# Weight rows of the first two chunks in even and odd order, and three late chunks in one load, in the opening of a two-problem attention kernel

## Chip, cores, metric

One core of a Trainium2 chip. The metric is the device time of one execution in microseconds (us); the median of several executions is given with its range. "Ratio" is the mean time of one kernel's fast runs over that of the kernel before in the same rounds, so it is not quite the ratio of the medians that are quoted. A profile is one execution, traced; its span is about 1.8 us shorter than the device time. Each ratio is taken within one session; where single traces are compared, they can be of different chips.

## The reference

Two independent problems A and B of one shape; the outputs are put side by side.

```
B, Sq, D = 16, 32, 1024
Hq, Hkv, Sk, Dh = 32, 4, 512, 128          # bf16
q = (x @ wq) as [B, Hq, Sq, Dh]            # wq: 1024 x 4096
scores = q k^T * Dh**-0.5 ; p = softmax(scores) ; o = p v
out = o @ wo                               # wo: 4096 x 1024
```

Only the product `x @ wq` of problem A, for its first eight heads, is touched here. It sums over the 1024 model dimensions in eight chunks of 128. Any assignment of dimensions to chunks gives the same sum, as long as x and wq use the same one.

## The kernel before

TensorE is kept busy nearly all the time by a plan in which scores, values and projections are woven together. What matters here is the opening, before that plan starts: while the first data arrive, eight heads are accumulated chunk by chunk in eight places of PSUM. x comes on two ways: its first 256 dimensions as they are, to be transposed by TensorE, the other 768 by transposing DMA loads.

```python
NF = REP - 2            # six heads first, two after them
HC = DC // 2            # 4 of the 8 chunks
wq_v = A_wq.rearrange("(c p) n -> p c n", p=P)
...
load_x(TT // 2, TT, nc.scalar)
nc.scalar.preload_act_table_set("natural_log_exp_and_others")
load_x(0, TT // 2)
load_w0(0, 1, 0, NF // 2)                  # chunk 0, three heads
load_w0(0, 1, NF // 2, NF, nc.scalar)      # chunk 0, three more
load_w0(1, 2, 0, NF)                       # chunk 1
load_w0(2, 3, 0, NF, nc.scalar)            # chunk 2
load_x_transposed(2)                       # x for chunks 2 and 3
load_w0(3, 4, 0, NF)
load_w0(0, HC, NF, REP)                    # chunks 0 to 3 of the last two heads
load_w0(HC, HC + 1, 0, REP)
load_x_transposed(HC)
load_w0(HC + 1, DC - 1, 0, REP)            # chunks 5 and 6
load_x_transposed(HC + 2)
load_w0(DC - 1, DC, 0, REP)                # chunk 7
...
warm_up(22)                                # matmuls on constants
for k, ts in enumerate(((0, TT // 2), (TT // 2, TT))):
    transpose_x(0, *ts, nc.vector.tensor_copy)
    transpose_x(1, *ts, nc.scalar.copy, spare[k])
for ts in ((0, TT // 2), (TT // 2, TT)):
    first_heads(range(0, NF // 2), (0,), *ts)
first_heads(range(NF // 2, NF), (0,))
first_heads(range(NF), (1, 2, 3))
first_heads(range(NF, REP), range(HC))
first_heads(range(REP), range(HC, DC - 1))
for n, h in enumerate((0, 2, 4, 6, 5, 7, 1, 3)):
    first_heads((h,), (DC - 1,))
    ...                                    # copy head h out of PSUM
```

## Time and profile before

| | kernel before |
|---|---|
| device time, median of the first three runs | 343.4 us (343.21 to 343.67) |
| span of the profiled execution | 341.1 us |
| TensorE busy | 334.5 us, 98% |
| chunk 1 issued, landed | 1.75, 6.23 us |
| first matmul of chunk 1 | 6.28 us |
| first matmul of the next heads (after the opening's 67) | 18.80 us |

How to read it: TensorE is the bound. The opening is the first 19 us. The prediction below shows the lines of the profile of before that carry this. A row of the timeline is start, duration, engine, source line, operation, and in brackets the idle time before it with what ended it.

### The profile page before, as it was taken

How to read it: one execution, taken by the hardware profiler on the slowest of the kernel's cores; microseconds unless marked ns; L12 is line 12 of the kernel's file. 1: busy time of each engine (PE TensorE's matmuls, PEld its weight loads, DVE VectorE, ACT ScalarE, POOL GpSimd, SP SyncE). 2: the span in 40 equal slices, each digit the busy share in tenths (PEclk: the TensorE clock that was granted, in tenths of full speed). 3: DMA queues.
4: the chain of work that ended last, by engine and by line, in shares of the span. 5: the costliest groups of instructions: out<-in, count | busy, mean ns of one | idle time of the engine just before them, and what ended most of it. 6: DMA issues, size and time to landing. Idle time of an engine off the chain costs nothing.

```text
span 341.1 us, 5436 instructions
## 1 busy us (share of the span) xinstructions
PE 334.5 (98%) x2074; PEld 212.8 (62%) x2113; DVE 265.4 (78%) x335; ACT 185.3 (54%) x208; POOL 47.0 (14%) x206
## 2 busy tenths in 40 slices
PE   8999999999999999999999999999999999999996
PEld 5455666666666666666666666666666666666555
DVE  0047988888988898888888988879888888889540
ACT  2057666666667667666645545555554555555110
POOL 0001110011111111110012221222122101111100
PEclk9999999999999999999999999999999999999999
DMA  7999999999996998899999955998449995430001
GB/s 199 298 188 274 288 250 225 205 254 250 301 258 144 241 222 232 197 294 308 322 293 290 240 125 147 338 284 222 118 106 307 357 194 152 115 93 9 17 19 33
DMA packets 128622, 71.70 MB, mean 210 GB/s; under 512 B 76880, under 2 KB 127824, under 8 KB 128592
## 3 DMA queue, kind: packets, MB, share of 16 engines
q1 hardware_dynamic: 127504, 69.78, 82.5%
q0 software_dynamic: 384, 1.05, 0.8%
q10 hardware_dynamic: 704, 0.49, 0.5%
q8 instruction: 17, 0.28, 0.3%
q14 instruction: 13, 0.11, 0.1%
HBM read 50.59 MB, written 2.10 MB: 154 GB/s over the span
## 4 chain that ended last, share of the span: by engine, by line
PE 96%; DMA 2%; issue 1%; ACT 0%; SPq 0%; ACTq 0%
PE f_ps L320 31%; PE q_ps L301 28%; PE ob L425 17%; PE s_ps L357 16%; PE q_ps L531 4%; DMA w_sb<-in_A_wq_dram 1%; DMA out_dram<-o_sb 0%; ACT o_sb L329 0%; SPq L465 0%; SPq L474 0%; ACTq L329 0%; ACT p_sb L365 0%; ACTq L365 0%
## 5 line engine op out<-in xcount | busy, mean ns | idle before, releaser
L365 ACT ACTIVATE p_sb<-s_ps,shift 128x1024 bf16<-128x1024 f32 x128 | 142.7, 1115 | 97.5 <-PE s_ps L357 86.3
L376 DVE TRANSPOSE_TENSOR_REDUCE parts<-p_sb 128x32 f32<-128x1024 bf16 x128 | 158.7, 1240 | 20.8 <-ACT p_sb L365 19.3
L320 PE MATMUL f_ps<-wo_sb,oT 128*128 128x512 bf16 (+1 forms) x524 | 127.6, 366 | 0.6
L301 PE MATMUL q_ps<-xT,wq_sb 128*128 128x512 bf16 x430 | 113.0, 379 | 0.6
L425 PE MATMUL ob<-p_sb,v_sb 128*128 128x256 bf16 x512 | 76.8, 273 | 0.8
L357 PE MATMUL s_ps<-qT,kT 128*128 128x256 bf16 x512 | 76.8, 273 | 0.0
L320 PEld LDWEIGHTS <-oT 128*128 128x128 bf16 x544 | 53.2, 98 | 35.3
L357 PEld LDWEIGHTS <-kT 128*128 128x128 bf16 x512 | 56.9, 113 | 28.3
L301 PEld LDWEIGHTS <-wq_sb 128*128 128x128 bf16 x448 | 43.8, 98 | 32.2
L425 PEld LDWEIGHTS <-v_sb 128*128 128x128 bf16 x512 | 50.1, 98 | 20.0
L447 DVE TENSOR_TENSOR oT<-r,ob 128x512 bf16<-128x512 f32 x64 | 43.9, 686 | 19.8 <-PE ob L425 19.4
L411 DVE STREAM_TRANSPOSE r<-rall 128x512 f32<-128x512 f32 x64 | 44.2, 691 | 1.1
L309 ACT CAST qT<-q_ps 128x512 bf16<-128x512 f32 x56 | 32.7, 583 | 16.5 <-PE q_ps L301 16.5
L394 POOL COPY half<-cs 64x32 f32<-64x32 f32 x32 | 6.6, 206 | 231.5 <-DVE cs L384 231.4
L329 ACT CAST o_sb<-f_ps 128x512 bf16<-128x512 f32 (+1 forms) x17 | 9.5, 559 | 23.6 <-PE f_ps L320 23.6
L531 PE MATMUL q_ps<-xT,w_sb 128*128 128x512 bf16 (+1 forms) x66 | 14.1, 369 | 0.6 <-DMA w_sb<-in_A_wq_dram 0.6
L406 DVE RECIPROCAL rall<-sums 128x32 f32<-128x32 f32 x32 | 10.4, 326 | 3.3 <-POOL sums L403 3.3
L384 DVE TENSOR_REDUCE cs<-parts 128x32 f32<-128x128 f32 x32 | 12.1, 377 | 1.1
L553 DVE CAST qT<-q_ps 128x512 bf16<-128x512 f32 x4 | 2.5, 683 | 13.2 <-PE q_ps L531 13.2
L531 PEld LDWEIGHTS <-w_sb 128*128 128x128 bf16 x67 | 6.4, 97 | 8.0 <-DMA w_sb<-in_A_wq_dram 1.1
L553 ACT CAST qT<-q_ps 128x512 bf16<-128x512 f32 x4 | 2.1, 599 | 12.8 <-PE q_ps L531 12.8
L331 POOL DMA_DIRECT2D out_dram<-o_sb x8 | 4.6, 575 | 29.2 <-ACT o_sb L329 29.2
(25 smaller groups left out, 48.1 us busy)
## 6 DMA issues: line engine op xcount, KB each, us to landing
v_sb<-in_A_v_cache_dram SPq DMA_DIRECT2D x16, 512.0 KB, 5.4
wq_sb<-in_B_wq_dram SPq DMA_DIRECT2D x8, 1024.0 KB, 6.0
wo_sb<-in_A_wo_dram SPq DMA_DIRECT2D x8, 1024.0 KB, 7.5
v_sb<-in_B_v_cache_dram SPq DMA_DIRECT2D x16, 512.0 KB, 4.6
wo_sb<-in_B_wo_dram SPq DMA_DIRECT2D x8, 1024.0 KB, 8.5
wq_sb<-in_A_wq_dram SPq DMA_DIRECT2D x5, 1024.0 KB, 6.7
wq_sb<-in_A_wq_dram SPq DMA_DIRECT2D x2, 512.0 KB, 7.3
kT<-in_A_k_cache_dram SPq DMA_TRANSPOSE x64, 4.4
```

The lines of the kernel that those rows point to most:

```text
L301: nc.tensor.matmul(ps[:], lhsT=w[:, dc, (h % 4) * DH:(h % 4 + 1) * DH], rhs=xT[pr][:, dc, :], start=(dc == 0), stop=(dc == DC - 1),)
L309: nc.scalar.copy(out=qT[pr, g][:, :, hl, :], in_=ps[:].rearrange("p (b s) -> p b s", s=SQ),)
L320: nc.tensor.matmul(ps[:, 0:width], lhsT=oT[pr, tt][:, h, :], rhs=wo_tiles[pr, nh, h // REP][:, h % REP, off:off + width], start=(h == 0), ...
L357: nc.tensor.matmul(s_ps[:, c, :], lhsT=kT[:, i % GRP, c, :], rhs=qT[pr, g][:, b, :, :].rearrange("p h s -> p (h s)"), start=True, stop=True,)
L365: nc.scalar.activation(out=p_sb[:], in_=s_ps[:], func=ACTF.Exp, bias=shift[:], scale=SCALE)
L376: nc.vector.tensor_reduce(out=parts[k][:, q, :, :].rearrange("p c h -> p (c h)"), in_=st[i]["p"][:].rearrange("p c (h s) -> p (c h) s", s=SQ),
L384: nc.vector.tensor_reduce(out=cs[:], in_=parts.pop(k)[:].rearrange("p q c h -> p q h c"), axis=AX.X, op=ALU.add,)
L406: nc.vector.reciprocal(out=rall[:, k, :], in_=quad.pop(k)[:])
L411: nc.vector.transpose(out=r[:].rearrange("p n s -> p (n s)"), in_=rall[:, k, o * 2 * REP:(o + 1) * 2 * REP] .unsqueeze(2).to_broadcast([P, ...
L425: nc.tensor.matmul(ob[j][:, q, :], lhsT=v_sb[:, i % GRP, c, :], rhs=st[i]["p"][:, c, :], start=(c == 0), stop=(c == KC - 1),)
L447: nc.vector.tensor_tensor(out=out, in0=rcp.pop(j)[:].rearrange("p (q h) s -> p q h s", h=REP), in1=ob.pop(j)[:].rearrange("p q (h s) -> p ...
L531: nc.tensor.matmul(first_q[h][:, ts], lhsT=w0[dc // HC][:, dc % HC, h * DH:(h + 1) * DH], rhs=xT[0][:, dc, ts], start=(dc == 0 and t0 == 0 ...
```

## The change

Intent: chunks 0 and 1 take the even and the odd ones of the first 256 dimensions, so that row 2p for chunk 0 and row 2p+1 for chunk 1 are neighbours in memory. x is transposed at a step of 2 to match. Besides, chunks 5, 6 and 7 come in one load, and the load of chunks 0 to 3 of the last two heads becomes two. So the whole program issues 176 DMA transfers before and after.

```diff
+            pair_v = A_wq[0:2 * P].rearrange("(p c) n -> p c n", c=2)
...
             def load_w0(d0, d1, h0, h1, eng=nc.sync):
+                rows = wq_v if d0 >= 2 else pair_v
...
-                    in_=wq_v[:, d0:d1, h0 * DH:h1 * DH],
+                    in_=rows[:, d0:d1, h0 * DH:h1 * DH],
...
-            load_w0(0, HC, NF, REP)
+            load_w0(0, 2, NF, REP)
+            load_w0(2, HC, NF, REP)
             load_w0(HC, HC + 1, 0, REP)
             load_x_transposed(HC)
-            load_w0(HC + 1, DC - 1, 0, REP)
+            load_w0(HC + 1, DC, 0, REP)
             load_x_transposed(HC + 2)
-            load_w0(DC - 1, DC, 0, REP)
...
-                        ps[:, tt * P:(tt + 1) * P], x_sb[:, tt, d * P:(d + 1) * P], ident[:]
+                        ps[:, tt * P:(tt + 1) * P], x_sb[:, tt, d:2 * P:2], ident[:]
```

## The prediction

> **What bounds the kernel now.** I read the page's busy shares and its chain first, then the opening of the program (the diff touches nothing else) as a timeline, then the chain of that stretch, the landings of its loads, and the stretch by windows.
>
> From the page of the kernel before:
>
> ```profile
> PE 334.5 (98%) x2074; PEld 212.8 (62%) x2113; DVE 265.4 (78%) x335; ACT 185.3 (54%) x208; POOL 47.0 (14%) x206
> ...
> PE 96%; DMA 2%; issue 1%; ACT 0%; SPq 0%; ACTq 0%
> ...
> L357 PEld LDWEIGHTS <-kT 128*128 128x128 bf16 x512 | 56.9, 113 | 28.3
> ...
> L425 PEld LDWEIGHTS <-v_sb 128*128 128x128 bf16 x512 | 50.1, 98 | 20.0
> ```
>
> TensorE is busy 98% of 341.1 us and is 96% of the chain that ended last. The change removes no matmul, so only waits of TensorE can be won. DMA is 2% of the chain; part of it is the output's end, the rest lies in the opening. The timeline of the opening (start, duration, engine, line, operation, count, idle before):
>
> ```profile
> 0.93 2.52 PE L513 MATMUL q_ps<-const-bfloat16-1.0 128*128 128x128 bf16 x22 [0.93 <-PEq L687]
> ...
> 1.26 0.92 SPq L474 DMA_DIRECT2D w_sb<-in_A_wq_dram  x2
> ...
> 1.34 0.94 ACTq L474 DMA_DIRECT2D w_sb<-in_A_wq_dram  x2
> 2.22 1.44 SPq L468 DMA_TRANSPOSE xT<-in_A_x_dram  x1
> ...
> 3.40 0.88 PE L521 MATMUL xT_ps<-ident,x_sb 128*128 128x128 bf16 x8
> ...
> 4.17 1.50 PE L531 MATMUL q_ps<-xT,w_sb 128*128 128x256 bf16 x9
> ...
> 6.27 12.20 PEld L531 LDWEIGHTS <-w_sb 128*128 128x128 bf16 x58 [1.09 <-DMA w_sb<-in_A_wq_dram]
> 6.28 12.69 PE L531 MATMUL q_ps<-xT,w_sb 128*128 128x512 bf16 x57 [0.59 <-DMA w_sb<-in_A_wq_dram]
> ```
>
> Chunk 0 of the weights (nine matmuls) is used up early; then TensorE waits once, for chunk 1, and never again in the opening. The 58 weight loads of the last rows belong to 58 matmuls (one record is missing), so one 512-wide matmul takes (12.69 - 0.16)/58 = 0.216 us, where 0.16 is what the last one's 0.38 us of latency has over the pace. The idle row shows 0.59 us against the modelled end of the matmul before. By the pace, the ninth started at 5.30 and its successor could have started at 5.52 instead of 6.28: the true loss is 0.76 us. The chain of the first 9 us says which load that is:
>
> ```profile
> 1.70 0.05 issue
> 1.75 4.48 DMA w_sb<-in_A_wq_dram
> 6.23 0.05 issue
> 6.28 2.33 PE q_ps L531 x10
> ```
>
> It is chunk 1 from the SyncE queue, 192 KB, issued at 1.75 and landed at 6.23. The DMA rows of single issues (KB, us to landing) for chunk 1 with chunk 2, the first transposing load of x (dimensions 2 and 3), and the present load of chunks 5 and 6:
>
> ```profile
> w_sb<-in_A_wq_dram SPq DMA_DIRECT2D x1, 192.0 KB, 4.5
> w_sb<-in_A_wq_dram ACTq DMA_DIRECT2D x1, 192.0 KB, 4.7
> ...
> xT<-in_A_x_dram SPq DMA_TRANSPOSE x1, 5.2
> ...
> w_sb<-in_A_wq_dram SPq DMA_DIRECT2D x1, 512.0 KB, 5.5
> ```
>
> Windows (length, busy time by engine, clock, DMA share, GB/s):
>
> ```profile
> 2.00:4.00 2.00, 2.00 (x20) 1.68 (x19) 0.17 (x1) 0.60 (x1) 0.00 (x0) 1.00 0.89 278
> 4.00:5.60 1.60, 1.60 (x14) 0.94 (x11) 0.41 (x2) 0.65 (x2) 0.00 (x0) 1.00 1.15 220
> 5.60:6.30 0.70, 0.10 (x2) 0.03 (x2) 0.00 (x0) 0.00 (x0) 0.00 (x0) 1.00 0.88 166
> 6.30:9.00 2.70, 2.65 (x12) 1.26 (x14) 0.00 (x0) 0.00 (x0) 0.00 (x0) 1.00 1.14 308
> 9.00:12.00 3.00, 3.00 (x16) 1.37 (x14) 0.00 (x0) 0.00 (x0) 0.00 (x0) 1.00 1.20 298
> ```
>
> The DMA engines have packets in flight all the time (share about 1), but the rate drops from 278 to 220 and 166 GB/s just where chunks 1 and 2 and the first transposing load are in flight. Packets wait there. That is the place the change may touch.
>
> **What the skill says.** (1) "DMA: Bandwidth & Descriptors", section "Issuing engines are not separate DMA queues": DMAs of SyncE and ScalarE interleave on the same 16 engines, only issue time is saved. The trace agrees: chunks 1 and 2, issued within 0.1 us of each other from two queues, land 0.27 us apart, both after over 4.4 us. (2) Same page, "Latency and other measured facts", on the row pitch in HBM at large powers of two: copies at a per-partition pitch of 512 KiB made 207 GB/s, at 2 MiB 164. The change takes the pitch of chunks 0 and 1 from 8 KiB (4096 bf16) to 16 KiB, far below these. The trace has only one pitch for these loads and doesn't settle it. (3) "SBUF — State Buffer", the note on cachelines of 16 bytes: a bf16 step up to 8 should be free. The trace differs slightly: weight loads of kT, read at a step of 4 elements, take 113 ns against 98 ns for v_sb, read in order.
>
> **The change part by part.**
> - Even and odd dimensions. The same 256 rows of wq are read, in the same 128 packets of 768 or 1536 bytes for each load; only which rows belong to which load changes. Even and odd rows stay separate slices of a row, so no packet gets longer. Work removed: none. If neighbouring rows are cheaper for the memory to serve, chunk 1 lands earlier than 6.23. Nothing in the trace measures that.
> - Transposes of x. Eight weight loads from x_sb now read at step 2. At most 113 - 98 = 15 ns each by the kT rows, 8 x 0.015 = 0.12 us, ahead of chunk 0. That delay falls into the 0.76 us wait for chunk 1: 0 on the path.
> - The load of the two last heads of chunks 0 to 3 is split in two: one more issue of about 0.5 us on SyncE (the row of 0.92 for two gives 0.46 each) at about 5 us. By the pace these heads are due at 6.28 + 18 x 0.216 = 10.16 and the load landed at 9.10. 0 on the path.
> - Chunks 5 to 7 in one load: one issue fewer, which gives the 0.5 us back before the next weight loads. But chunk 5 now waits for chunk 7's 256 KB too: 262,144 B at 298 GB/s = 0.88 us, so 12.33 + 0.88 = 13.21, against a need at 6.28 + 34 x 0.216 = 13.62. It holds by 0.41 us; with the extra issue's 0.5 us in full it would be late by about 0.1 us. The third transposing load, behind it, goes from 13.28 to some 14.2, needed at 15.35. Chunk 7 goes from 15.44 to 13.2, needed at 17.08. Nothing of that is won, as it was not waited for.
> - Sum of the sure parts: 0.0 us. The open part is the 0.76 us wait.
>
> **How much of the 0.76 us can be had.** After chunk 1 come six matmuls, so chunk 2 is due at 6.28 + 6 x 0.216 = 7.57. Chunk 2 landed at 6.50, but its x at 7.39 (issued at 2.22, 5.18 us): only 0.18 us of slack. If chunk 1 alone comes early, the gain stops at 0.18 us and the wait moves to xT. For more, the transposing load must come earlier too, which it may if the packets ahead of it in the same queue stall less. Then 0.66 us of slack at chunk 3 (8.21 against 8.87) and 0.41 us at chunks 5 to 7 come next. A gain of 0.4 us would already be a good outcome.
>
> **Rivals.**
> A. Neighbours help: chunk 1 lands by about 5.5, the transposing load advances some. For: the rate dip to 220 and 166 GB/s says that the memory or the queues, and not the bytes, hold it up. Against: all packets are the same size and number, and the dip also coincides with the start of the transposing load, which stays. Time: 342.7 to 343.2.
> B. Nothing moves, or the wait passes to xT after 0.18 us: 343.2 to 343.4. For: the same bytes, queues and order of issue up to 4.8 us.
> C. The wider pitch hurts, or the odd rows collide with chunk 2, which is read beside them: chunk 1 later by 0.3 to 0.5 us, loss one for one: 343.7 to 343.9. For: this wait has no slack at all. Against: 16 KiB is still a small pitch.
> D. Chunks 5 to 7 late by 0.1 to 0.3 us: 343.5 to 343.7.
>
> **Range and chances.** I give A 0.4, B 0.35, C 0.15 and D 0.1. Weighted with 342.95, 343.3, 343.8 and 343.6 the mean is 343.3; as A's gain is what the change is made for, and its tail is longer, I say 343.2 us. The three runs before span 0.46 us by themselves, so the range is 342.5 to 343.9. 2% is 6.9 us; the opening's whole wait is 0.76 us. Faster by over 2%: 0.005; slower: 0.005; within: 0.99.
>
> **What would show it.** In the chain of the first 9 us the DMA piece ahead of the first long run of matmuls tells all: its end at 6.23 moves earlier in A (and a second wait, for xT at about 7.3, appears if only chunk 1 moved), stays in B, is later in C. D shows as an idle of TensorE near 13.6 us. The eight transposes should take 0.88 to 1.0 us. From 24 us on, every row should be the old one shifted by the same amount. I am wrong if the body's pace changes, or if the opening moves by more than 0.8 us.

## The result, and the profile after

343.28 us median of 6 runs (342.95 to 343.62) against 343.31 us of before (342.94 to 343.67, 6 runs); ratio 0.9999, 95% interval 0.9986 to 1.0011. No difference.

The page of the changed kernel, engines and chain, as before:

```profile
PE 335.0 (98%) x2074; PEld 213.2 (62%) x2113; DVE 265.4 (78%) x335; ACT 185.4 (54%) x208; POOL 47.1 (14%) x206
...
PE 96%; DMA 2%; issue 1%; ACT 0%; SPq 0%; ACTq 0%
```

The chain of the first 24 us of the changed kernel (start, duration, what):

```profile
1.75 4.80 DMA w_sb<-in_A_wq_dram
6.56 0.05 issue
6.60 2.33 PE q_ps L533 x10
```

The same load as before sets the start of the long run of matmuls. In this execution it landed at 6.56, 0.33 us later than in the profile of before. From there on every weight load of TensorE is later by 0.327 or 0.328 us: the body of the kernel has no slack and adds no noise.

The timeline of the changed kernel, TensorE's rows of the opening:

```profile
3.40 1.04 PE L523 MATMUL xT_ps<-ident,x_sb 128*128 128x128 bf16 x8
...
4.23 2.03 PE L533 MATMUL q_ps<-xT,w_sb 128*128 128x256 bf16 x9
...
6.60 12.69 PE L533 MATMUL q_ps<-xT,w_sb 128*128 128x512 bf16 x57 [0.34 <-DMA w_sb<-in_A_wq_dram]
```

The 57 recorded matmuls take the same 12.69 us as before. But the nine of chunk 0 took 2.03 us in place of 1.50, and TensorE's idle time before chunk 1 is 0.34 in place of 0.59 us. TensorE was slower, and waited less. This was in no step of the prediction, and it turned out to be half of the story.

The windows of the changed kernel for the stretch in which the rate of the DMA dropped before (columns as in the prediction):

```profile
4.00:5.60 1.60, 1.60 (x12) 1.23 (x10) 0.41 (x2) 0.75 (x2) 0.00 (x0) 1.00 0.92 218
5.60:6.30 0.70, 0.66 (x4) 0.10 (x1) 0.00 (x0) 0.00 (x0) 0.00 (x0) 1.00 1.13 160
```

218 and 160 GB/s against 220 and 166: in this execution the dip is where it was. It is not in every execution, though: in the second looks (next section) the same two stretches moved 287 and 271 GB/s in the changed kernel, 240 and 116 in the kernel before. In the experiments with one part alone it was 238 and 67 with even and odd rows, 241 and 68 with rows in turn. So the dip changes from execution to execution in both forms, and neighbouring rows do not lift it dependably.

### The profile page after: what moved, and what is told of

Same layout as the page of the kernel before. It is cut to its first block, busy times and chain, and to the rows that moved or that the text cites. A ratio compares the mean times of both kernels' runs of the same rounds, so it can differ in the third digit from the quotient of the medians.

```text
span 341.5 us, 5438 instructions
## 1 busy us (share of the span) xinstructions
PE 335.0 (98%) x2074; PEld 213.2 (62%) x2113; DVE 265.4 (78%) x335; ACT 185.4 (54%) x208; POOL 47.1 (14%) x206
## 4 chain that ended last, share of the span: by engine, by line
PE 96%; DMA 2%; issue 1%; ACT 0%; SPq 0%; ACTq 0%
PE f_ps L320 31%; PE q_ps L301 28%; PE ob L425 17%; PE s_ps L357 16%; PE q_ps L533 4%; DMA w_sb<-in_A_wq_dram 1%; DMA out_dram<-o_sb 0%; ACT o_sb L329 0%; SPq L466 0%; SPq L476 0%; ACTq L329 0%; ACT p_sb L365 0%; ACTq L365 0%
```

## The experiments

Theories: (1) neither part of the change touches what sets the end; chunk 1's landing scatters by itself. (2) The change itself delays chunk 1 by 0.3 us. (3) Two effects cancel. Later: what holds chunk 1 up, and what else bounds the opening (theory C, TensorE's pace).

All "full pace" times below are read from the starts of single matmuls in the trace, to about 0.1 us: 512 columns are 0.427 us apart at first ("half pace") and 0.216 us later, and the time is that at which the distance changes.

### Both kernels looked at again

No edit.

> The kernel before, unchanged, looked at once more. Theory 1 (the 0.3 us by which the changed kernel's first chunk-1 load landed later is chance): chunk 1 lands anywhere from 6.1 to 6.7 us, not at 6.23 again, and the first late matmul follows it by 0.05 us. Theory 2 (the change itself delays chunk 1): it lands at 6.2 to 6.3 again. Time 342.9 to 343.7 us either way.

> The changed kernel, unchanged, looked at once more. Theory 1 (chance): chunk 1 lands anywhere from 6.1 to 6.7 us. Theory 2 (the change delays it): 6.5 to 6.6 again. Time 342.9 to 343.7 us.

Measured: 343.25 and 343.36 us, one run each, so of unknown state. The kernel before again landed chunk 1 at 6.23 us, which theory 1 had ruled out in so many words ("not at 6.23 again") and theory 2 had asked for. The changed kernel landed it at 5.41 us, against 6.56 the first time, earlier than the range that I had given for chance. Theory 2 is out, as its own kernel lands both earlier and later than before; and the unchanged rows, too, landed chunk 1 anywhere from 5.99 to 6.79 us in the experiments below. The scatter is wider than I thought. And though chunk 1 came 0.82 us earlier than in the kernel before, the next heads began later: 19.26 us in place of 18.80. Chunk 1 (SPq) and chunk 2 (ACTq) in the DMA rows of that look (KB, us from issue to landing), and TensorE's timeline:

```profile
w_sb<-in_A_wq_dram SPq DMA_DIRECT2D x1, 192.0 KB, 3.7
w_sb<-in_A_wq_dram ACTq DMA_DIRECT2D x1, 192.0 KB, 3.8
```

```profile
4.10 15.32 PE L533 MATMUL q_ps<-xT,w_sb 128*128 128x256 bf16 x67
...
14.06 0.98 PEld L533 LDWEIGHTS <-w_sb 128*128 128x128 bf16 x6 [0.35 <-DMA w_sb<-in_A_wq_dram]
```

There is no wait for chunk 1 at all, yet the 67 matmuls are not done earlier. Why, shows in the durations (minimum, median, maximum in ns) of the matmuls from 5.0 to 6.5 us of the same execution:

```profile
L533 PE MATMUL q_ps<-xT,w_sb x6: 417/524/632, 4.7 to 6.2; 128*128 128x256 bf16 x3, 128*128 128x512 bf16 x3
```

A 512-wide matmul takes up to 632 ns here, in the body 379. The column of the granted clock does not show it; the window from 4.5 to 6.0 us of this execution (columns as before, the clock is third from the end) says 1.00 with eight matmuls in 1.5 us:

```profile
4.50:6.00 1.50, 1.50 (x8) 0.88 (x6) 0.00 (x0) 0.21 (x1) 0.00 (x0) 1.00 1.27 288
```

The reason lies in the view: it subtracts only what is on record as lost, and this trace's first clock record, of the full clock, starts at 6.76 us; before that there is none, and the view prints 1.00. In eleven of the thirteen traced attention kernels the first record starts within about 0.1 us of the change of pace (3.95 us in the first profile of before, 5.38 in that of after); the second look at before and the run with chunk 2 away from chunk 1 have no clock record at all.

TensorE ran at half its pace until 6.85 us. In the first profile of before it was at full pace from 3.9 us on, in that of after from 5.4 us. That the row at 14.06 us waited for the load of chunks 5 to 7 (landed at 14.02) is rival D of the prediction; it cost 0.02 us, the distance of 0.235 us between two matmuls less the pace of 0.216.

In the second look at the kernel before, the wait sat elsewhere again (full pace from about 5.6 us):

```profile
9.09 9.61 PEld L531 LDWEIGHTS <-w_sb 128*128 128x128 bf16 x46 [0.55 <-DMA w_sb<-in_A_wq_dram]
```

Chunk 3, which had 0.66 us of slack in the first profile, landed at 9.04 and was the last to be waited for.

### Each part alone

```diff
# even and odd alone: the diff above, without this part of it:
-            load_w0(HC + 1, DC - 1, 0, REP)
+            load_w0(HC + 1, DC, 0, REP)
...
-            load_w0(DC - 1, DC, 0, REP)
# late load alone: that part only
```

> The even and odd dimensions alone, chunks 5 and 6 and chunk 7 loaded as before. Theory 1 (neither part touches the path): ratio to before 0.999 to 1.001, chunk 1 at 6.1 to 6.7 us, the load of chunks 5 and 6 lands at 12.2 to 12.9 us. Theory 3 (two effects cancel: the rows help by some 0.3 us and the late load costs as much): ratio 0.999 or less, below that of the late load alone by 0.001 or more.

> The three late chunks in one load alone, rows as before. Theory 1: ratio 0.999 to 1.001, no idle of TensorE at chunk 5; the load lands at 13.0 to 13.6 us, against a need that is 7.35 us after the first matmul of chunk 1. Theory 3 (cancelling): an idle of TensorE near 13.6 us and a ratio of 1.001 or more.

Measured: even and odd alone 343.56 us (343.12 to 343.93, 5 runs), ratio 1.0003, 0.9990 to 1.0017; chunk 1 landed at 6.70 us, chunks 5 and 6 at 12.38 us. Late load alone 343.25 us (342.71 to 343.66, 5 runs), ratio 0.9995, 0.9981 to 1.0008; chunk 1 at 6.79 us, the late load at 13.05 us, and no idle of TensorE there. Theory 3 needed the reverse order, the rows below and the late load above 1, and that was not seen. But the two ratios are not quite comparable. Even and odd alone keeps the split of the last two heads' load without the merged late load, so it issues 177 transfers in place of 176, and its trace is 0.43 us longer after the last matmul, for a reason that has nothing to do with the rows (below, after the table of the openings). Less these 0.43 us (0.0013) its ratio would be about 0.9990. Neither part has an effect that these runs resolve. An effect under some 0.15% (0.5 us) can't be excluded by the ratios alone, which is why the rows were measured by themselves, too.

### The rows by themselves

A kernel of loads only. Its output is wrong, which doesn't matter for the time.

```python
rows = {
    "in_turn": wq.rearrange("(c p) n -> p c n", p=P),
    "even_odd": wq[0:2 * P].rearrange("(p c) n -> p c n", c=2),
    "every_8th": wq.rearrange("(p c) n -> p c n", c=8),
}
for k in range(3):                        # 30 rounds, other columns in each
    name = ("in_turn", "even_odd", "every_8th")[(n + k) % 3]
    ...
    nc.sync.dma_start(out=zeroth[:], in_=rows[name][:, 0, cols])
    nc.sync.dma_start(out=first[:], in_=rows[name][:, 1, cols])
    nc.scalar.dma_start(out=second[:], in_=rows["in_turn"][:, 2, cols])
    ...                                   # VectorE reads all three
```

> Wrong result on purpose, and no attention at all: only loads. 90 bursts, each of chunk 0 and chunk 1 of the query weights (192 KB each, rows of 1536 B) from SyncE and chunk 2 from ScalarE, as in the opening but without x; the next burst waits for the last. The three forms of chunks 0 and 1 (rows in turn, even and odd rows, rows 8p and 8p+1) take turns, 30 bursts each. Theory N (neighbouring rows are cheaper): chunk 1's median time to landing is shorter by 0.1 us or more for even and odd rows than for rows in turn. Theory P (a wider pitch costs): longer by 0.1 us or more for even and odd rows, and more for rows 8p. Theory 0 (which rows makes no difference): medians within 0.1 us of each other.

Measured, in one execution: time to landing of chunk 1 (us, minimum, median, maximum; 30 loads each), for rows in turn, then even and odd, then 8p and 8p+1:

```profile
DMA to landing us min/median/max: 2.7/3.2/3.9
```

```profile
DMA to landing us min/median/max: 2.9/3.1/3.9
```

```profile
DMA to landing us min/median/max: 3.0/3.4/4.8
```

The medians are 3.19, 3.08 and 3.42 us, the means 3.14, 3.13 and 3.43. Rows in turn against even and odd: 0.10 us by the median, which just meets the bound that I had set for theory N, and 0.01 us by the mean, with standard deviations of 0.25 and 0.19. So theory N is not shown: the loads can't be told apart, and a gain would be of 0.1 us or so, on a load whose landing scatters by more. Rows 8p at a pitch of 64 KiB do cost, 0.23 us by the median, and chunk 0 of the same bursts is later by about as much. So which rows are read can matter, but no such effect shows at the step that was made here. The bursts are less crowded than the opening (3.1 to 3.2 us to landing in place of 3.7 to 5.0), so an effect that needs the loads of x beside it is not excluded by them; the landings in the kernels themselves overlap (5.99 to 6.79 us in turn, 5.41 to 6.70 even and odd).

In the kernel itself, with the same 8p rows (wrong; on top of even and odd alone):

```diff
-            pair_v = A_wq[0:2 * P].rearrange("(p c) n -> p c n", c=2)
+            pair_v = A_wq.rearrange("(p c) n -> p c n", c=8)
```

> Wrong result on purpose: as the even and odd dimensions alone, but chunks 0 and 1 read rows 8p and 8p+1, a pitch of 64 KiB in place of 16 KiB. If the row pitch matters for these loads, chunk 0 (4.05 us) or chunk 1 lands later by 0.3 us or more than in the even and odd form. If it doesn't, chunk 0 lands at 4.0 to 4.2 us and chunk 1 at 6.1 to 6.7 us; ratio 0.999 to 1.001.

Measured: 343.56 us (343.36 to 343.93, 4 runs), ratio 1.0008, 0.9992 to 1.0023 (with the same 0.43 us of the 177th transfer in it); chunk 0 landed at 4.03 us and chunk 1 at 6.81. One more landing at the late end; the measurement with 30 loads each is the one to go by. (The comparison with the reference passed this and the next kernel, although both compute other sums than they should: it is no evidence about them.)

### The wait taken away

Chunk 1's matmuls take chunk 0's weights.

```diff
-                            lhsT=w0[dc // HC][:, dc % HC, h * DH:(h + 1) * DH],
+                            lhsT=w0[dc // HC][:, 0 if dc == 1 else dc % HC, h * DH:(h + 1) * DH],
```

> Wrong result on purpose: the matmuls of chunk 1 take chunk 0's weights, so TensorE no longer waits for chunk 1; all loads stay. By the prediction's slack sum only 0.18 us of the 0.76 us can be had, as chunk 2's x lands at 7.4 to 7.7 us and TensorE would wait for it: TensorE goes from chunk 0 to chunk 1 without a gap, then waits for xT until 7.4 to 7.7 us; from there it is 0.1 to 0.3 us ahead of the kernel before; ratio 0.9990 to 0.9998. Rival: the transposing load is not the next limit, and 0.6 us or more is won, ratio 0.9983 or less.

Measured: 342.69 us (342.55 to 343.17, 5 runs) against 343.23, ratio 0.9989, 0.9975 to 1.0003. The chain of the first 24 us of this kernel:

```profile
4.35 2.83 PE q_ps L531 x15
7.18 0.03 issue
7.21 11.38 PE q_ps L531 x52
```

15 matmuls run through, then TensorE waits for x of chunk 2, landed at 7.17 us (the distance of two matmuls here is 0.41 us, 0.19 more than the pace). The next heads start at 18.43 us, 0.37 us ahead of the first profile of before. So the order of the waits was as the prediction had it, with a gain of 0.37 us in the trace in place of 0.1 to 0.3, because the transposing load landed 0.22 us earlier in this execution. The ratio lies between what both sides expected, closer to the first, and its interval still touches 1. This is the estimate of what anything that only speeds up chunk 1 can bring: about 0.1% of the time, and by the interval not over 0.25%.

### What holds chunk 1 up

```diff
# chunk 2 away from chunk 1
-            load_w0(2, 3, 0, NF, nc.scalar)
             load_x_transposed(2)
+            load_w0(2, 3, 0, NF)
# the transposing load behind chunk 3
-            load_x_transposed(2)
             load_w0(3, 4, 0, NF)
+            load_x_transposed(2)
```

> Chunk 2 goes from the ScalarE queue to SyncE behind the transposing load, so that no other weight load is in flight beside chunk 1. If chunk 1 is held up by sharing the engines with chunk 2 (theory Q), it lands by 5.2 to 5.6 us and chunk 2 at 8 us or later, for which TensorE waits. If it is held up by the start of the transposing load (theory T), it lands at 5.9 to 6.5 us as before.

> The transposing load of x goes behind chunk 3's load on the same queue. If its start holds chunk 1 up (theory T), chunk 1 lands by 5.0 to 5.6 us. If chunk 2 beside it does (theory Q), chunk 1 still lands at 5.9 to 6.5 us. Either way the x of chunk 2 comes at about 8 us and TensorE waits for it; the time is up by 0.3 to 1.0 us.

Measured, one run each: with chunk 2 away, 343.31 us and chunk 1 at 5.70 us; with the transposing load later, 343.29 us and chunk 1 at 6.05 us, with x of chunk 2 at 7.74. Theory T expected chunk 1 by 5.6 in the second, and it landed at 6.05; but the edit only moved the issue of the transposing load from 2.22 to 2.69 us, so it was still on its way beside chunk 1, and T is not excluded. For theory Q, 5.70 is just outside what it expected and inside what chance does to chunk 1 with chunk 2 beside it (5.41 to 6.79). One look at each can't settle it: what holds chunk 1 up stays open. The time did not rise in the second, either, against what I expected: TensorE was at half pace until 6.65 us there and used the time up. In the first, TensorE waited for chunk 2 as expected (landed at 7.92 us, a little before the 8 us).

### The pace

```diff
-            warm_up(22)
+            warm_up(0)
```

> The 22 matmuls that only warm TensorE up are left out, all else as before. Theory C (the opening is bound as much by the time at which TensorE gets to its full pace as by chunk 1): the pace of 0.107 us for 256 columns comes 1 to 2.5 us later than with them (3.9 to 7.1 us so far), the next heads start at 19.5 to 20.6 us, ratio 1.002 to 1.005. Rival (chunk 1 alone binds): the next heads start at 18.8 to 19.4 us, ratio 0.9990 to 1.0010.

Measured: 344.17 us (343.36 to 344.5, 6 runs) against 343.19, ratio 1.0023, 1.0011 to 1.0035. Full pace came at 8.85 us (1.8 us after the latest with the warm-up), the next heads started at 20.28 us: theory C by all three numbers. The chains of the first 24 us, this kernel first, then the changed kernel's second look:

```profile
4.33 16.12 PE q_ps L531 x67
20.45 3.45 PE q_ps L301 x16
```

```profile
4.30 15.12 PE q_ps L533 x67
19.42 3.45 PE q_ps L301 x16
```

Chunk 1 landed at 6.70 us without the warm-up, no later than in the late load alone (6.79), whose profiled execution made 343.66 us against 344.5 here. In both the whole opening ran as a chain of matmuls, without the warm-up a full microsecond longer. The Trainium skill, "TensorE: Matmul & The Clock Gate", section "Part 1: The HAM clock gate", tells of an activity window of about 3.4 us that runs freely and does not start with the kernel; these traces agree in that the same 22 matmuls from 0.93 us on were followed by full pace anywhere from 3.9 to 7.0 us, and that without them it came later than in any of these.

### Two tries at a better kernel

Chunk 1 split by heads over both queues; chunk 2 behind it on ScalarE, and in the second try on SyncE ahead of the transposing load.

```diff
-            load_w0(1, 2, 0, NF)
+            load_w0(1, 2, 0, NF // 2)
+            load_w0(1, 2, NF // 2, NF, nc.scalar)
             load_w0(2, 3, 0, NF, nc.scalar)        # second try: load_w0(2, 3, 0, NF)
```

> A version meant to be better: chunk 1 is split by heads over the SyncE and the ScalarE queue, chunk 2 goes behind on ScalarE. Chunk 1 should land at 5.2 to 6.0 us instead of 6.2 to 6.8. The run without the wait has the ceiling: it started the next heads at 18.43 us in the profile (18.80 to 19.49 in the others) and made 0.9989. So the ratio is expected at 0.9988 to 0.9998; 1.0000 or more if chunk 2 or its x becomes the wait, or if TensorE is still at half its pace then.

> The split of chunk 1 once more, with ScalarE left at its three issues: chunk 2 goes on SyncE, ahead of the transposing load. Split over both queues with a fourth issue on ScalarE was slower (1.0024) though its profiled execution was one of the fast ones (343.11 us); there ScalarE's last issue started at 3.79 instead of 2.28 us and stood in front of its copies of x. Theory S (that issue on ScalarE is what made the other executions slow): now 0.9985 to 1.0000, chunk 1 at 5.2 to 6.0 us, and TensorE waits for x at 7.2 to 7.8 us at most. Rival (the split itself costs, by more loads or by putting the transposing load back): 1.001 or more again.

Measured: the first 344.03 us (343.11 to 344.37, 6 runs), ratio 1.0024, 1.0012 to 1.0036; the second 343.68 us (343.15 to 343.94, 5 runs), ratio 1.0009, 0.9995 to 1.0022. The first is a miss: chunk 1 landed at 5.61 and 5.86 us as hoped, and the profiled execution started the next heads at 18.56 us and was one of the two fast ones (343.11 us), but four of six runs took 343.9 to 344.4 us. What the trace of the fast one shows is a cause to suspect:

```profile
1.35 2.78 ACTq L474 DMA_DIRECT2D w_sb<-in_A_wq_dram  x3
...
4.17 0.67 ACT L526 COPY xT<-xT_ps 128x256 bf16<-128x256 bf16 x2 [1.57 <-PE xT_ps L522]
```

ScalarE's three issues end at 4.13 us in place of 2.28 us for two (2.28 is their end, and not a start as the expectation has it), and its copies of x stand behind them. Without the fourth load on ScalarE the ratio fell to 1.0009, but that is not the 1.0000 or less that theory S asked for, and its interval takes in both. Both tries also issue one transfer more than before, which costs 0.43 us (0.0013) at the end of their traces (next section). Less that, the second would be at about 0.9996, as theory S had it, and the first still at about 1.0011. Why the first was slow in most executions stays open. Neither beats the other two kernels as it stands.

## Why the prediction was right

The opening of all profiled kernels comes out of two terms. Either the last load that is waited for sets the start of the next heads: landing, 0.05 us, and the matmuls that remain at 0.2157 us. Or the pace does: the 67 matmuls need 6 x 0.109 + 61 x 0.2157 = 13.81 us at full pace, and each microsecond at half pace adds half of one. The numbers are from single records of the traces.

| kernel, execution | full pace from | last load waited for | by the load | by the pace | measured start |
|---|---|---|---|---|---|
| before, first | 3.9 | chunk 1, 6.23 | 6.28 + 58 x 0.2157 = 18.79 | 17.99 | 18.80 |
| before, second | 5.6 | chunk 3, 9.04 | 9.09 + 46 x 0.2157 = 19.01 | 18.66 | 19.03 |
| after, first | 5.4 | chunk 1, 6.56 | 6.61 + 12.51 = 19.12 | 18.62 | 19.13 |
| after, second | 6.85 | none but 0.02 us | - | 4.10 + 13.81 + 1.38 = 19.29 | 19.26 |
| late load alone | 7.0 | chunk 1, 6.79 | 6.84 + 12.51 = 19.35 | 4.32 + 13.81 + 1.34 = 19.47 | 19.49 |
| chunk 1 not waited for | 4.6 | x of chunk 2, 7.17 | 7.22 + 52 x 0.2157 = 18.44 | 18.19 | 18.43 |
| no warm-up | 8.85 | chunk 1, 6.70 | 6.75 + 12.51 = 19.26 | 4.12 + 13.81 + 2.37 = 20.30 | 20.28 |

The other six profiled attention kernels fit to 0.02 us as well, four by the load that was waited for last, the one with the transposing load later by the pace, and the second try at a split by x of chunk 2.

The end follows the start: from the start of the next heads to the last matmul it is 318.96 us in all thirteen. What comes after that has two lengths. With 175 or 176 transfers in the program the span ends 322.32 to 322.38 us after the start of the next heads; with 177 (even and odd alone, rows 8p, both tries) 322.75 or 322.76. The instruction records show where the 0.43 us lie: SyncE ends the program with a list of waits for the semaphores that count the transfers, about 0.06 us each, and the transfers take these semaphores in turn. With 176 the last output's semaphore is in the last wait of the list, so this one alone is left when the output has landed; with 177 the turn has come round to an earlier semaphore, and eight waits are left. So the one transfer more cost these four kernels about as much as the whole wait for chunk 1 was worth (0.37 us above).

Point by point:

- TensorE is the bound, and "only waits of TensorE can be won": right; the shift of the opening is carried to the end unchanged.
- The sum of 0.0 us for the sure parts: right within what the runs resolve (1.0003 and 0.9995 for the parts alone).
- The transposes at a step of 2: right that they cost nothing on the path. The check that I gave, 0.88 to 1.0 us for the eight, failed: they took 1.04 us. The step is not the reason, since the unchanged kernel's second look, at half pace, took 1.06 us at a step of 1. Nor do the runs bear out the 15 ns that the prediction put on the step: the eight weight loads took 102 to 152 ns at a step of 2 in the first profile of after, and 98 to 152 ns at a step of 1 in that of before.
- Chunks 5 to 7 by 13.21 us, against a need 7.34 us after the first matmul of chunk 1: right in kind, under-sized. They landed at 13.60 us (needed at 13.94), 14.02 (a loss of 0.02) and, in the late load alone, 13.05 (needed at 14.2). The slack of 0.41 us was in truth anything from 1.1 us down to nothing.
- The slack of 0.18 us behind chunk 1, with x of chunk 2 as the next wait: right in order, and shown by the kernel that does not wait for chunk 1.
- The rivals: B's time is what was measured, though the prediction gave A the higher chance (0.4 against 0.35). Its number lay between the two and was off by 0.1 us; the range, 342.5 to 343.9 us, took in all four rivals, so neither speaks for a mechanism. A's, that neighbours are cheaper to read, is not shown: 0.01 us by the mean, 0.10 by the median of 30 loads. C's does not show at 16 KiB, either; at 64 KiB it costs 0.23 us by the median. In the first profile chunk 1 was late by 0.33 us, which C would have claimed, and in the second early by 0.82 us, which A would have: both were chance.
- What failed is a premise of the sum and not a term: that TensorE is at its full pace whenever it has its data, so that a delay of chunk 1 is a "loss one for one" because "this wait has no slack at all". The wait of 0.76 us is not a fixed reserve. It is what is left of the time to chunk 1 when TensorE happens to get to its full pace early. In the four traces with full pace at 6.65 us or later TensorE lost at most 0.06 us to chunk 1, so there was nothing to shorten. Both, the landing (5.41 to 6.79 us for the unsplit load beside chunk 2) and the pace (3.9 to 7.0 us), change from execution to execution, and the larger one wins. The start of the next heads differs by 0.46 us in the four looks at the two unchanged kernels alone (18.80 to 19.26), so this can make up a good part of the range of before over all runs, 342.64 to 343.71 us, of which the prediction had seen only 0.46 us. It may be all of it: the spans of the runs of before in the experiments' rounds are 340.7 to 341.8 us, and less the 322.33 us of the traces that leaves 18.4 to 19.5 us for the start of the next heads, an estimate that meets the 18.43 to 19.49 us of the traces with the warm-up.

## What to carry to other kernels

A wait in one profile is one draw: look at the same kernel twice before sizing a gain from it, above all in the first microseconds. Where two things overlap (a load on its way, an engine not yet at its pace), removing one is worth only the part by which it exceeds the other, and that part may be there in some executions alone. Changing which rows go to which load, with packets of the same size and number, bought nothing that could be measured here; 30 loads of each form by themselves said so more sharply than any timing of the whole. Keep the number of transfers the same when two kernels are compared for a few tenths of a microsecond, or look at what their ends cost: one transfer more was 0.43 us here.

## What the Trainium skill lacked or had wrong

- "TensorE: Matmul & The Clock Gate", section "Part 1: The HAM clock gate": its example has the change of pace around 4 us into sustained matmuls, within 0.5 us from run to run. Here, after the same warm-up from 0.93 us on, full pace came between 3.9 and 7.0 us, a spread of 3.1 us. That fits the section's freely running window of 3.4 us and its remark that the number of slow matmuls varies by run, and not the 0.5 us. (The matmuls here did not run unbroken: the transposes and short waits stand between.)
- Same section, on the clock events of a trace, which it calls unreliable on trn2: here eleven of thirteen traces have a first event within about 0.1 us of the change of pace, and two have none. The page does not say that events can be missing altogether. A mean made of the events alone reads 1.00 where there are none, as it did from 4.5 to 6.0 us in the second look at the changed kernel, before its first event at 6.76 us. The pace of the matmuls is the safer thing to read.
- Same page, "Part 4: PE-mode transpose": it says that the full clock doesn't engage for transposes. If that means that transposes run at half pace, the first profile of before differs: the last of its eight transposes started 0.056 us after the one before it, and 0.107 us was the distance at half pace. If it means that transposes don't bring the full clock on, no run here tells, as none has transposes alone.
- "DMA: Bandwidth & Descriptors", "Latency and other measured facts": the row pitch in HBM is told from 512 KiB up. For loads of 192 KB in 1536 B rows, 16 KiB made no difference that matters against 8 KiB (3.08 and 3.19 us to landing), and 64 KiB cost 0.23 us (3.42 us).
- No page has the scatter of a single load in a crowded opening: chunk 1's 192 KB, issued at 1.75 us, landed between 5.99 and 6.79 us with rows in turn (six traces, chunk 2 beside it) and between 5.41 and 6.70 us with even and odd rows (three traces).
